# Attention scores gathered ten equally spaced query rows at a time, nine of them used, in blocks of 18 rows

## The chip, the cores and the metric

The kernel runs on one core of a Trainium2 chip. The core has five engines that run side by side and wait for each other by semaphores: TensorE (PE; its weight loads are listed apart as PEld), VectorE (DVE), ScalarE (ACT), GpSimd (POOL) and SyncE (SP). SP computes nothing here: it issues all the transfers, in order, and sixteen DMA engines carry them out. The metric is the device time of one launch in microseconds, lower is better.

## The reference

There are an attention layer whose heads are mixed before and after the softmax, and two expert layers without routing. All is float32; the weights arrive as float64.

```
# B, H, S, D = 4, 12, 448, 64
scores = q @ k.T / sqrt(D)                          # per batch and head
scores = einsum('bhij,hg->bgij', scores, w_pre)     # premix of the heads
attn = exp(scores - max(scores)); attn /= (sum(attn) + 1e-9)
attn = einsum('bhij,hg->bgij', attn, w_post)        # postmix of the heads
x = (attn @ v), heads side by side                  # 1792 tokens x 768
h = x @ w_in;  x = (h * clip(h + 3, 0, 6) / 6) @ w_out          # 768 -> 2048 -> 768
out = ((x @ w1) * (x @ w2)) @ w3 @ moe2_w_out                    # 768 -> 1024 -> 1024 -> 768
```

## The kernel before

Attention goes batch by batch, and in a batch by four chunks of query rows (`CHUNKS`: 120, 100, 116 and 112 rows). `scores` computes a chunk two heads at a time; the result is copied to the tile `s`, in which a partition is a query row and the free dimension is the head and the key. The premix sums over heads, so the heads must come to lie on partitions. That is what the gather is for: a DMA from SBUF to SBUF that takes some query rows of `s`, each with its 12 heads, and lays every pair of row and head on a partition of its own of the tile `g`. One gather of the kernel before takes five rows (four in the short blocks) at equal distance, which is 60 (48) rows of 448 numbers. Four such gathers make a block of 20 (16) query rows: two halves `a_` on the partitions from 0 and from 64 (`PIECE`), and two sides `y` in the free dimension. There are 23 blocks a batch, 92 in all.

In each block `mix(s)` does this. `premix` multiplies the four pieces with `wih`, which holds w_pre on the diagonal of the five rows (`SET`). `rowmax` on DVE takes the maximum, and two exponentials on ACT (`softexp`) write `e` and the sums `z`. `guard`, `recip` and `weigh` scale the postmix weights by one over the sum. `postmix` applies them, with the keys now on partitions (32 small matmuls), and two copies (`evac`, line 283 on DVE, line 281 on ACT) bring the result to `pt`. After two chunks `values` multiplies `pt` with v and stores x in DRAM. The tiles `g`, `e` and the PSUM tiles each have four buffers.

Every engine's order is made by a planner (class `Plan`) while the program is built: each operation has a priority, a guessed duration and its dependencies, and the planner lets every engine take the most urgent operation that is ready in its own list schedule. The numbers that set these priorities stand in `URGE`: `gather=-66.75`, for example, is how far ahead of the block's nominal time (`s * unit0`) a gather stands, and the `p...` numbers say when a second engine may take work of the first. The plan is fixed after that; on the chip each engine works through its list.

The first expert layer begins as the last batch's attention ends. Its weights are loaded by SP, converted from float64 on ACT and DVE, and split into a high and a low part; three matmuls (`product`) make one of float32 precision. Then come the product of w3 and w4 (tile names `w`, `w34`) and the second expert layer (`up`, `down`). All matmuls are issued from line 211, so rows are told apart by their tiles: `sc` scores, `pre` premix, `post` postmix, `val` values, `up` and `dn` the layers.

Of the kernel before, what the change touches and what calls it, by code (L numbers as in the profile page):

```python
# [26 lines left out]

SET = 5
ROWS = 12 * SET
CHUNKS = [[20] * 6, [20] * 5, [20] * 5 + [16], [20] * 4 + [16] * 2]  # L30
LEN = [sum(c) for c in CHUNKS]
CH0 = [sum(LEN[:c]) for c in range(4)]
WIDE = [20 * len(c) for c in CHUNKS]
# [9 lines left out]

def query_order():

    order = np.full(WD0[4], -1)
    for c, blocks in enumerate(CHUNKS):
        c0 = CH0[c]
        for t, n in enumerate(blocks):
            order[WD0[c] + t + len(blocks) * np.arange(n)] = c0 + np.arange(n)  # L50
            c0 += n
    return order
# [3 lines left out]
URGE = dict(pPool=56.7, pACT=727.19, pDVE=31.92, pOut=15.85, pGuard=161.57, pCopy=49.01, pRest=2.09, pEvac=23.46, load0=8.42, load=-2.09, gather=-66.75, pre=-9.2, max=-4.2, exp=24.45, norm=3.85, post=2.04, evac=32.9, values=15.38, step=14.3, vload=27.62, vload0=-34.83, lead=-26.96, begin=-9.0, consts=-93.5, moe=64.56, rows=1.62, win=-43.78, wout=-28.18, w34=16.61, w2=-8.59, unit0=3.751, unit1=12.228, unit2=10.914, w34us=69.106)  # L56
# [146 lines left out]
def attention_moe(ctx: ExitStack, tc, qd, kd, vd, consts, w_in, w_out, w1, w2, w3t, w4, out):  # L203
# [20 lines left out]
    def pool(name, side=left, **kw):  # L224
# [18 lines left out]
        "consts": (cp, [128, 2 * H + SET], F32, 1),  # L243
# [26 lines left out]
    for b in range(B):  # L270
        for c in range(4):
            cstart.append(len(slots))
            for t in range(len(CHUNKS[c])):
                unit_of.append(2 * b + c // 2)
                slots.append((b, c, t))
# [20 lines left out]
    def constants():  # L296
        raw = Buf("consts")
        dma_in(URGE["consts"], consts, raw, ns=300)

        def emit():  # L300
            x = raw.t
            own = x[:, 2 * H:]
# [4 lines left out]
            nc.vector.tensor_tensor(  # L307
                out=wip, in0=x[:, H:2 * H].unsqueeze(2).to_broadcast([128, H, SET]),
                in1=own.unsqueeze(1).to_broadcast([128, H, SET]), op=ALU.mult)
        plan.add("DVE", 700, -6, emit, use=(raw,))  # L310
# [44 lines left out]
    def mix(s):  # L355

        at = s * U0
        b, c, t = slots[s]
        ng, n = len(CHUNKS[c]), CHUNKS[c][t] // 4
        K = 12 * n  # L360
        st = stile[4 * b + c]
        g, pre, m, e, z, r, w, post = (Buf(x) for x in ("g", "pre", "m", "e", "z", "r", "wt", "post"))
        new = [g]
        for a_ in range(2):
            def gather(a_=a_):
                if a_ == 0:
                    take(g)
                for y in range(2):
                    p0 = t + ng * n * (2 * y + a_)
                    nc.sync.dma_start(out=g.t[PIECE * a_:PIECE * a_ + K, y], in_=st.t[p0:p0 + ng * (n - 1) + 1:ng])  # L370
            op = plan.add("SP", 1400, at + URGE["gather"], gather, read=(st,), new=new, after=g.writers[:1], hold=(g,))
            if a_:
                g.writers.append(op)
            new = []
# [7 lines left out]
        plan.add("PE", 950, at + URGE["pre"], premix, use=(g,), new=(pre, e))  # L382
# [37 lines left out]
        def postmix():  # L420
            take(post, *dest)
            for a_ in range(2):
                for k, k0 in enumerate(KEY0):
                    for y in range(2):
                        i, o = slice(PIECE * y, PIECE * y + K), slice(k % 2 * PIECE, (k % 2 + 1) * PIECE)
                        c0 = 256 * a_ + k // 2 * ROWS
                        mm(post.t[o, y, c0:c0 + ROWS], e.t[i, a_, k0:k0 + PIECE], w.t[i, a_], True, True)
        op = plan.add("PE", 1000, at + URGE["post"], postmix, use=(e, w), new=(post, *dest), hold=(pt,), after=() if first else (pt.first,))
        if first:
            pt.first, pt.writers = op, []  # L430

        c0 = CH0[c] - CH0[c // 2 * 2] + sum(CHUNKS[c][:t])
# [5 lines left out]
        for y in range(2):  # L438
            op = plan.add({"ACT": 575, "DVE": 645}, 0, at + URGE["evac"], lambda eng, y=y: evac(eng, y), read=(post,), hold=(pt,), wait="Evac")
# [429 lines left out]
```

## Time and profile before

| what | value |
|---|---|
| time, median of 3 runs | 1405.83 us (1399.33 to 1406.45) |
| the profiled execution | 1406.89 us |
| its span, first to last instruction | 1405.1 us |
| mean granted TensorE clock | 0.967 of full speed |
| PE busy | 1299.0 us, 92% of the span |
| DVE, ACT, POOL busy | 66%, 33%, 26% |
| DMA: moved, share of the 16 engines on the one hardware queue | 155.38 MB, 34.9% |

The shares are averages over unlike stages: attention up to some 430 us, the first expert layer to some 980, then the product of w3 and w4, and the second expert layer. A busy share of PE counts a matmul as long as its record lasts, so it isn't the share of its peak. The DMA share is the mean over sixteen engines: a transfer that sits on a few of them can hold those fully busy and still show as a small share.

### The profile page before, as it was taken

What the parts mean: (1) busy time and instruction counts of PE and PEld (TensorE: products, weight loads), DVE (VectorE), ACT (ScalarE), POOL (GpSimd) and SP (SyncE); (2) the same over time, 40 slices, a digit from 0 to 9 for tenths busy, and PEclk for the clock granted to TensorE, in tenths of its full rate; (3) what the DMA queues carried; (4) which work ended last, traced back from release to release, by engine and by line L of the source; (5) the groups of instructions that cost most, each with busy time, mean ns of one, the idle gap of its engine ahead of it and who ended that gap; (6) DMA issues with size and microseconds to landing.
All of it is one profiled execution on the core that took longest, in us unless ns stands there. A gap on an engine that the chain in (4) does not pass through costs nothing.

```text
span 1405.1 us, 29332 instructions
## 1 busy us (share of the span) xinstructions
PE 1299.0 (92%) x12192; PEld 1040.2 (74%) x12192; DVE 931.4 (66%) x1550; ACT 469.8 (33%) x905; POOL 362.2 (26%) x313
## 2 busy tenths in 40 slices
PE   5898988999889698999999998999998999999998
PEld 2444554555456597888988887998887899999997
DVE  1655656556667698898898989556725665656433
ACT  4544445445445443223222222223314211111110
POOL 0000000000023644343443433323433222222210
PEclk8999999999999799999999999999999999999999
DMA  5354554444455543333233423111623121111004
GB/s 211 134 160 152 157 167 156 153 156 152 155 179 171 186 146 97 107 91 126 91 97 95 123 91 98 53 38 57 192 97 135 46 57 46 45 35 45 23 5 153
DMA packets 75413, 157.26 MB, mean 112 GB/s; under 512 B 7184, under 2 KB 40976, under 8 KB 75280
## 3 DMA queue, kind: packets, MB, share of 16 engines
q1 hardware_dynamic: 75280, 155.38, 34.9%
q8 instruction: 96, 1.57, 0.5%
q14 instruction: 37, 0.30, 0.1%
HBM read 95.32 MB, written 21.50 MB: 83 GB/s over the span
## 4 chain that ended last, share of the span: by engine, by line
PE 43%; DMA 24%; DVE 17%; issue 9%; POOL 4%; SPq 2%; ACT 2%; POOLq 0%; ACTq 0%; DVEq 0%
PE up L211 18%; DMA g<-s 15%; PE dn L211 12%; PE w L211 3%; DVE raw L563 3%; PE pre L211 3%; PE val L211 3%; DVE raw L567 3%; DMA raw<-w 3%; DMA raw<-w_in 2%; PE sc L211 2%; DVE raw L559 2%; DVE raw L565 2%; SPq L370 2%; PE post L211 2%
## 5 line engine op out<-in xcount | busy, mean ns | idle before, releaser
L211 PE MATMUL up<-act,w 128*128 128x448 f32 x2304 | 491.3, 367 | 11.2 <-ACT act L281 3.6
L211 PEld LDWEIGHTS up<-act,w 128*128 128x128 f32 x2304 | 432.7, 189 | 51.5 <-ACT act L281 4.0
L211 PE MATMUL dn<-gs,w 128*128 128x448 f32 x1728 | 384.3, 374 | 31.3 <-POOL gs L214 10.5
L211 PEld LDWEIGHTS dn<-gs,w 128*128 128x128 f32 x1728 | 330.5, 192 | 68.1 <-POOL gs L214 13.9
L652 DVE TENSOR_TENSOR acc<-acc,dn 128x896 f32<-128x896 f32 x168 | 181.4, 1083 | 86.3 <-PE dn L211 83.1
L214 POOL TENSOR_TENSOR gs<-t,gs 128x448 fp32r<-128x448 f32 (+1 forms) x60 | 103.1, 1719 | 316.8 <-ACT gs L281 300.5
L211 PE MATMUL pre<-g,wih 60*64 60x448 f32 (+1 forms) x736 | 138.7, 574 | 36.7 <-DMA g<-s 36.4
L214 POOL TENSOR_TENSOR w<-raw,w 128x768 fp32r<-128x768 f32 (+1 forms) x63 | 125.6, 1995 | 169.7 <-ACT w L281 74.0
L386 DVE TENSOR_REDUCE m<-pre 128x2 f32<-128x896 f32 x92 | 99.7, 1085 | 85.9 <-PE pre L211 85.9
L553 ACT ACTIVATE raw<-raw 128x384 f32<-128x384 f32 (+1 forms) x144 | 75.3, 528 | 241.2 <-DMA raw<-w 102.2
L392 ACT ACTIVATE e<-pre,m 128x448 f32<-128x448 f32 x184 | 115.6, 634 | 83.6 <-DVE m L386 66.0
L211 PEld LDWEIGHTS post<-wt,e 60*64 60x64 f32 (+1 forms) x5888 | 103.2, 136 | 50.8 <-issue 29.3
L211 PE MATMUL post<-wt,e 60*64 60x60 f32 (+1 forms) x5888 | 111.4, 222 | 10.0 <-issue 4.1
L559 DVE TENSOR_SCALAR raw<-raw 128x384 f32<-128x384 f32 (+1 forms) x144 | 78.6, 550 | 63.2 <-ACT raw L553 61.9
L397 POOL TENSOR_SCALAR z<-z 128x2 f32<-128x2 f32 x91 | 19.6, 215 | 391.1 <-ACT e L392 385.7
L283 DVE COPY pt<-post 128x480 f32<-128x480 f32 (+1 forms) x112 | 69.7, 640 | 47.1 <-ACT pt L281 34.7
L281 ACT CAST gs<-t 128x448 fp32r<-128x448 f32 (+1 forms) x59 | 43.6, 739 | 168.3 <-DVE t L809 124.8
L567 DVE SCALAR_TENSOR_TENSOR raw<-raw 128x384 f32<-128x384 uint32 (+1 forms) x144 | 95.4, 666 | 1.2
L211 PEld LDWEIGHTS pre<-g,wih 60*64 60x64 f32 (+1 forms) x736 | 32.3, 137 | 82.7 <-DMA g<-s 73.7
L211 PE MATMUL val<-pt,v 128*64 128x220 f32 (+1 forms) x768 | 88.0, 387 | 4.3 <-ACT e L392 3.3
L563 DVE SCALAR_TENSOR_TENSOR raw<-raw 128x384 int32<-128x384 int32 (+1 forms) x144 | 90.8, 632 | 1.5
L211 PE MATMUL sc<-k,q 64*120 64x448 f32 (+1 forms) x384 | 85.1, 574 | 6.8 <-DMA k<-kd 5.1
(47 smaller groups left out, 1004.1 us busy)
## 6 DMA issues: line engine op xcount, KB each, us to landing
g<-s SPq DMA_DIRECT2D x320, 105.0 KB
raw<-w SPq DMA_DIRECT2D x48, 384.0 KB
v<-vd SPq DMA_DIRECT2D x24, 512.0 KB
raw<-w_in SPq DMA_DIRECT2D x32, 384.0 KB
raw<-w_out SPq DMA_DIRECT2D x32, 384.0 KB
raw<-w3t SPq DMA_DIRECT2D x32, 256.0 KB
raw<-w4dram SPq DMA_DIRECT2D x16, 384.0 KB
k<-kd SPq DMA_DIRECT2D x12, 448.0 KB
```

The source lines that it names most:

```text
L211: nc.tensor.matmul(o, lhsT=lt, rhs=rh, start=start, stop=stop)
L214: eng.tensor_tensor(out=o, in0=a, in1=b, op=ALU.subtract)
L281: nc.scalar.copy(o, i)
L283: nc.vector.tensor_copy(o, i)
L370: nc.sync.dma_start(out=g.t[PIECE * a_:PIECE * a_ + K, y], in_=st.t[p0:p0 + ng * (n - 1) + 1:ng])
L386: nc.vector.tensor_reduce(out=m.t, in_=pre.t[:, :, :S], axis=AX.X, op=ALU.max, negate=True)
L392: nc.scalar.activation(out=e.t[:, a_], in_=pre.t[:, a_, :S], func=ACTF.Exp, bias=m.t[:, a_:a_ + 1], accum_out=z.t[:, a_:a_ + 1])
L553: nc.scalar.mul(value()[:, halves[i]], f(bits(i))[:, :, 1], 2.0 ** -112)
L559: one(out=f(y), in0=f(y), scalar1=F64_TOP, scalar2=-F64_TOP, op0=ALU.min, op1=ALU.max)
L563: two(out=y, in0=hi, scalar=-0x80000000, in1=y, op0=ALU.bitwise_and, op1=ALU.bitwise_or)
L567: two(out=f(hi), in0=lo, scalar=2.0 ** -52, in1=f(hi), op0=ALU.mult, op1=ALU.mult)
L652: nc.vector.tensor_tensor(out=o(), in0=o(), in1=p.t[:, :, :S], op=ALU.add)
```

## The change

A gather now takes ten equally spaced query rows, 120 rows of `g` in one transfer, and the block has two gathers, one for each side `y`. The first five rows lie on partitions 0 to 59. The sixth row (partitions 60 to 71) lies across the border at partition 64 and isn't used by this group; the last four lie on partitions 72 to 119. `wih` gets weights of zero for the sixth row, and the second half of a premix takes partitions 64 to 119. So one group (`GROUP`) is nine query rows, and a block 18. There are 50 groups a batch (the last two have eight rows each), 25 blocks a batch and 100 in all. The distance of the ten rows is the number of groups in the chunk less one (`APART`); by this the sixth row of one group belongs to another: the last group of a chunk, which lies at distance one, is made of the sixth rows (`group_rows`, `query_order`). The chunks have 12, 12, 13 and 13 groups, with 110, 110, 120 and 120 partitions of `s`, and since 37 isn't even, one block a batch takes its two sides from different chunks. The evacuation is cut by half `a_` (five rows of both sides, then four) instead of by side, and its second copy depends on its first in the plan. All numbers of `URGE` have been fitted anew, so the order of every engine changes.

```diff
-CHUNKS = [[20] * 6, [20] * 5, [20] * 5 + [16], [20] * 4 + [16] * 2]
...
+GROUP = 9
+GROUPS = [12, 12, 13, 13]
+APART = [g - 1 for g in GROUPS]
+G0 = [sum(GROUPS[:c]) for c in range(5)]
+BLOCKS = G0[4] // 2
+LEN = [GROUP * g for g in GROUPS[:3]]
+LEN.append(S - sum(LEN))
+WIDE = [10 * d for d in APART]
...
+def group_rows(c, t):
+
+    d = APART[c]
+    return (t, d) if t < d else (5 * d, 1)
...
-URGE = dict(pPool=56.7, pACT=727.19, pDVE=31.92, pOut=15.85, pGuard=161.57, pCopy=49.01, pRest=2.09, pEvac=23.46, load0=8.42, load=-2.09, gather=-66.75, pre=-9.2, max=-4.2, exp=24.45, norm=3.85, post=2.04, evac=32.9, values=15.38, step=14.3, vload=27.62, vload0=-34.83, lead=-26.96, begin=-9.0, consts=-93.5, moe=64.56, rows=1.62, win=-43.78, wout=-28.18, w34=16.61, w2=-8.59, unit0=3.751, unit1=12.228, unit2=10.914, w34us=69.106)
+URGE = dict(pPool=7.45, pACT=670.88, pDVE=510.18, pOut=3.51, pGuard=166.84, pCopy=16.72, pRest=14.77, pEvac=68.05, load0=23.0, load=2.97, gather=-94.67, pre=-13.63, max=-7.21, exp=31.46, norm=6.61, post=2.04, evac=23.77, values=15.1, step=14.3, vload=26.5, vload0=-31.32, lead=-23.93, begin=-9.6, consts=-84.7, moe=45.4, rows=18.18, win=-57.59, wout=-32.41, w34=9.23, w2=4.11, unit0=3.845, unit1=9.887, unit2=10.428, w34us=65.661)
...
-        for a_ in range(2):
-            def gather(a_=a_):
-                if a_ == 0:
+        for y in range(2):
+            G = 2 * t + y
+            c = next(c for c in range(4) if G < G0[c + 1])
+            p0, d = group_rows(c, G - G0[c])
+            st = stile[4 * b + c]
+
+            def gather(y=y, st=st, p0=p0, d=d):
+                if y == 0:
                     take(g)
-                for y in range(2):
-                    p0 = t + ng * n * (2 * y + a_)
-                    nc.sync.dma_start(out=g.t[PIECE * a_:PIECE * a_ + K, y], in_=st.t[p0:p0 + ng * (n - 1) + 1:ng])
-            op = plan.add("SP", 1400, at + URGE["gather"], gather, read=(st,), new=new, after=g.writers[:1], hold=(g,))
-            if a_:
+                nc.sync.dma_start(out=g.t[:120, y], in_=st.t[p0:p0 + 9 * d + 1:d])
+            op = plan.add("SP", 1250, at + URGE["gather"], gather, read=(st,), new=() if y else (g,), after=g.writers[:1], hold=(g,))
+            if y:
                 g.writers.append(op)
...
                 for a_ in range(2):
-                    i, o = slice(PIECE * a_, PIECE * a_ + K), slice(PIECE * y, PIECE * (y + 1))
+                    i, o = slice(PIECE * a_, 120 if a_ else ROWS), slice(PIECE * y, PIECE * (y + 1))
                     mm(pre.t[o, a_, :S], wih[i], g.t[i, y], True, True)
...
-        def evac(eng, y):
-            o = pt.t[:, :, c0 + 2 * n * y:c0 + 2 * n * (y + 1)].rearrange("p c (a i) -> p a c i", a=2)
-            i = post.t[:, y].rearrange("p (a x) -> p a x", a=2)[:, :, :JC * ROWS].rearrange("p a (c i) -> p a c i", i=SET)
-            copy(eng, o, i[:, :, :, :n])
+        def evac(eng, a_):
+            size = GROUP - (t == BLOCKS - 1)
+            n = size - SET if a_ else SET
+            o = pt.t[:, :, c0:c0 + 2 * size].rearrange("p c (y i) -> p y c i", y=2)[:, :, :, SET * a_:SET * a_ + n]
+            i = post.t[:, :, 256 * a_:256 * a_ + JC * ROWS].rearrange("p y (c i) -> p y c i", i=SET)[:, :, :, :n]
+            copy(eng, o, i)
...
+    p = np.arange(128)
+    own = np.where(p < ROWS, p // H, np.where((p < 72) | (p >= 120), -1, (p - 72) // H))
+    own2 = np.where(p % PIECE < ROWS, p % PIECE // H, -1)
```

On SP, in the middle of the first batch, the queue before reads as follows; `g<-s 60x1x448` is a gather of five rows, `x6` six transfers one after the other, and `q`, `k`, `v` are loads from DRAM.

```order
L293 DMA q<-qd 128x600
L370 DMA g<-s 60x1x448 x12
L293 DMA k<-kd 128x896
L370 DMA g<-s 60x1x448 x6
L293 DMA k<-kd 128x896
L370 DMA g<-s 48x1x448 x2
L293 DMA q<-qd 128x720
L370 DMA g<-s 60x1x448 x2
```

At the same place the changed kernel has:

```order
L305 DMA q<-qd 128x660
L381 DMA g<-s 120x1x448 x7
L305 DMA k<-kd 128x896
L381 DMA g<-s 120x1x448 x4
L305 DMA k<-kd 128x896
L381 DMA g<-s 120x1x448 x2
L305 DMA q<-qd 128x720
L305 DMA k<-kd 128x896
```

Of 22 gathers 13 are left in this piece; the loads stand in the same order among them, and the third k load now comes directly behind the q load.

On PE, where attention ends and the first up-projections (`up`) begin, the queue before is this, `pre` and `post` being the mixes of the last blocks and `val` the values:

```order
L211 MATMUL val<-pt,v 64x220 x8
L211 MATMUL up<-act_5607,w 128x448 x6
L211 MATMUL post<-wt,e 64x60 x32
L211 MATMUL up<-act_5607,w 128x448 x6
L211 MATMUL pre<-g,wih 64x448 x4
L211 MATMUL up<-act_5607,w 128x448 x3
```

In the changed kernel it is this:

```order
L224 MATMUL val<-pt,v 64x216 x8
L224 MATMUL pre<-g,wih 64x448 x4
L224 MATMUL post<-wt,e 64x60 x32
L224 MATMUL up<-act_5765,w 128x448 x3
L224 MATMUL pre<-g,wih 64x448 x4
L224 MATMUL up<-act_5765,w 128x448 x6
L224 MATMUL post<-wt,e 64x60 x32
L224 MATMUL up<-act_5765,w 128x448 x3
```

A block's matmuls are the same ones in both (four premixes, 32 postmixes); the up-projections still fill the gaps between the last blocks, now in smaller pieces.

## Rows read from the trace of the kernel before

**Rows 1.** The page: span, and the DMA share in 40 equal slices (tenths).

```profile
span 1405.1 us, 29332 instructions
DMA  5354554444455543333233423111623121111004
```

**Rows 2.** Windows: busy us (instructions) of each engine, granted clock, DMA share, GB/s.

```profile
13.00:427.00 414.00, 364.70 (x7392) 201.09 (x7392) 244.06 (x446) 208.58 (x493) 25.69 (x94) 0.93 0.49 158
50.00:400.00 350.00, 315.97 (x6508) 174.13 (x6508) 210.66 (x383) 176.45 (x415) 16.39 (x77) 0.95 0.49 156
250.00:275.00 25.00, 23.76 (x574) 14.82 (x570) 15.82 (x32) 13.85 (x31) 1.06 (x5) 0.97 0.48 155
300.00:325.00 25.00, 25.00 (x515) 14.87 (x514) 15.27 (x29) 12.83 (x29) 1.06 (x5) 0.88 0.44 142
500.00:880.00 380.00, 358.49 (x1708) 324.03 (x1707) 344.95 (x612) 109.61 (x169) 148.44 (x99) 0.98 0.34 104
```

**Rows 3.** The chain that ended last, by line, as shares of the span.

```profile
PE up L211 18%; DMA g<-s 15%; PE dn L211 12%; PE w L211 3%; DVE raw L563 3%; PE pre L211 3%; PE val L211 3%; DVE raw L567 3%; DMA raw<-w 3%; DMA raw<-w_in 2%; PE sc L211 2%; DVE raw L559 2%; DVE raw L565 2%; SPq L370 2%; PE post L211 2%
```

**Rows 4.** The chain from 200 to 300 us: shares, and one piece (start, us).

```profile
by line: DMA g<-s 47.1%; PE pre L211 12.9%; PE sc L211 10.6%; SPq L370 10.0%; PE val L211 9.4%; PE post L211 8.5%; issue 1.9%; SPq L293 0.5%
...
237.51 8.62 DMA g<-s
```

**Rows 5.** Premix weight loads: the group, and waits from 10 to 60 us.

```profile
L211 PEld LDWEIGHTS pre<-g,wih 60*64 60x64 f32 (+1 forms) x736 | 32.3, 137 | 82.7 <-DMA g<-s 73.7 <-issue 3.1 <-DVE wt L408 2.0
...
PEld pre L211 <- DMA g<-s: 16.3, 12, 8.0
```

**Rows 6.** Windows of the opening loads and of the first gathers.

```profile
0.00:13.00 13.00, 7.86 (x32) 4.03 (x34) 0.42 (x3) 6.38 (x8) 0.19 (x4) 1.00 0.86 306
26.00:32.00 6.00, 6.00 (x29) 1.74 (x26) 3.18 (x4) 2.06 (x6) 0.21 (x1) 0.69 0.33 121
```

**Rows 7.** Timeline of premix weight loads: start, us, what, idle before and releaser.

```profile
26.36 0.29 PEld L211 LDWEIGHTS pre<-g,wih 60*64 60x64 f32 x4 [0.61 <-DMA g<-s]
27.24 0.29 PEld L211 LDWEIGHTS pre<-g,wih 60*64 60x64 f32 x4 [0.59 <-DMA g<-s]
```

**Rows 8.** Gathers: SP's issues (ns min/median/max), then transfers by size.

```profile
L370 SPq DMA_DIRECT2D g<-s x368: 633/742/1071, 13.1 to 427.3; - x184
...
g<-s SPq DMA_DIRECT2D x320, 105.0 KB
...
g<-s SPq DMA_DIRECT2D x48, 84.0 KB
```

**Rows 9.** The chain: two loads from DRAM, one among gathers, one after them.

```profile
315.70 7.53 DMA q<-qd
...
450.96 3.98 DMA v<-vd
```

**Rows 10.** SP's issues in the chain: a gather of 48 rows, a q load.

```profile
210.42 0.63 SPq L370
...
211.84 0.42 SPq L293
```

**Rows 11.** SP's own waits from 50 to 400 us: total us, times, longest.

```profile
SPq L370 <- DMA g<-s: 28.6, 71, 1.1
```

**Rows 12.** The chain: one block's postmix and one premix on PE.

```profile
271.07 1.09 PE post L211 x64
272.16 0.88 PE pre L211 x8
```

**Rows 13.** Evacuations on DVE by form: busy us, mean ns, idle before.

```profile
L283 DVE COPY pt<-post 128x480 f32<-128x480 f32 x95 | 60.7, 655 | 37.5 <-ACT pt L281 27.6 <-PE post L211 9.6
...
L283 DVE COPY pt<-post 128x384 f32<-128x384 f32 x17 | 9.0, 554 | 9.6 <-ACT pt L281 7.1 <-PE post L211 2.5
```

More of the change, by code (lines that the diff above doesn't have):

```diff
@@ L41 @@
 F64_TOP = float(np.array(0x0FEFFFF0, np.uint32).view(np.float32))
+def group_rows(c, t):
+    d = APART[c]
+    return (t, d) if t < d else (5 * d, 1)
 def query_order():
     order = np.full(WD0[4], -1)
[L47 to L51, printed above, removed]
+    for c in range(4):
+        for t in range(GROUPS[c]):
+            first, d = group_rows(c, t)
+            G = G0[c] + t
+            for i, r in enumerate((0, 1, 2, 3, 4, 6, 7, 8, 9)[:GROUP - (G >= G0[4] - 2)]):
+                order[WD0[c] + first + d * r] = GROUP * G - (G == G0[4] - 1) + i
     return order
-URGE = dict(pPool=56.7, pACT=727.19, pDVE=31.92, pOut=15.85, pGuard=161.57, pCopy=49.01, pRest=2.09, pEvac=23.46, load0=8.42, load=-2.09, gather=-66.75, pre=-9.2, max=-4.2, exp=24.45, norm=3.85, post=2.04, evac=32.9, values=15.38, step=14.3, vload=27.62, vload0=-34.83, lead=-26.96, begin=-9.0, consts=-93.5, moe=64.56, rows=1.62, win=-43.78, wout=-28.18, w34=16.61, w2=-8.59, unit0=3.751, unit1=12.228, unit2=10.914, w34us=69.106)
+URGE = dict(pPool=7.45, pACT=670.88, pDVE=510.18, pOut=3.51, pGuard=166.84, pCopy=16.72, pRest=14.77, pEvac=68.05, load0=23.0, load=2.97, gather=-94.67, pre=-13.63, max=-7.21, exp=31.46, norm=6.61, post=2.04, evac=23.77, values=15.1, step=14.3, vload=26.5, vload0=-31.32, lead=-23.93, begin=-9.6, consts=-84.7, moe=45.4, rows=18.18, win=-57.59, wout=-32.41, w34=9.23, w2=4.11, unit0=3.845, unit1=9.887, unit2=10.428, w34us=65.661)
 SHARED = dict(
@@ L270, in attention_moe @@
     for b in range(B):
[L271 to L275, printed above, removed]
+        cstart += [b * BLOCKS + g // 2 for g in G0[:4]]
+        for t in range(BLOCKS):
+            unit_of.append(2 * b + (2 * t >= G0[2]))
+            slots.append((b, t))
     U0 = URGE["unit0"]
@@ L301, in emit @@
             x = raw.t
-            own = x[:, 2 * H:]
+            own, own2 = x[:, 2 * H:2 * H + SET], x[:, 2 * H + SET:]
             nc.vector.memset(wih[:, ROWS:], 0.0)
@@ L308, in emit @@
                 out=wip, in0=x[:, H:2 * H].unsqueeze(2).to_broadcast([128, H, SET]),
-                in1=own.unsqueeze(1).to_broadcast([128, H, SET]), op=ALU.mult)
+                in1=own2.unsqueeze(1).to_broadcast([128, H, SET]), op=ALU.mult)
         plan.add("DVE", 700, -6, emit, use=(raw,))
@@ L379, in premix @@
                 for a_ in range(2):
-                    i, o = slice(PIECE * a_, PIECE * a_ + K), slice(PIECE * y, PIECE * (y + 1))
+                    i, o = slice(PIECE * a_, 120 if a_ else ROWS), slice(PIECE * y, PIECE * (y + 1))
                     mm(pre.t[o, a_, :S], wih[i], g.t[i, y], True, True)
-        plan.add("PE", 950, at + URGE["pre"], premix, use=(g,), new=(pre, e))
+        plan.add("PE", 900, at + URGE["pre"], premix, use=(g,), new=(pre, e))
         def rowmax():
@@ L424, in postmix @@
                     for y in range(2):
-                        i, o = slice(PIECE * y, PIECE * y + K), slice(k % 2 * PIECE, (k % 2 + 1) * PIECE)
+                        i, o = slice(PIECE * y, PIECE * y + ROWS - 12 * a_), slice(k % 2 * PIECE, (k % 2 + 1) * PIECE)
                         c0 = 256 * a_ + k // 2 * ROWS
                         mm(post.t[o, y, c0:c0 + ROWS], e.t[i, a_, k0:k0 + PIECE], w.t[i, a_], True, True)
-        op = plan.add("PE", 1000, at + URGE["post"], postmix, use=(e, w), new=(post, *dest), hold=(pt,), after=() if first else (pt.first,))
+        op = plan.add("PE", 1020, at + URGE["post"], postmix, use=(e, w), new=(post, *dest), hold=(pt,), after=() if first else (pt.first,))
         if first:
             pt.first, pt.writers = op, []
-        c0 = CH0[c] - CH0[c // 2 * 2] + sum(CHUNKS[c][:t])
-        def evac(eng, y):
-            o = pt.t[:, :, c0 + 2 * n * y:c0 + 2 * n * (y + 1)].rearrange("p c (a i) -> p a c i", a=2)
-            i = post.t[:, y].rearrange("p (a x) -> p a x", a=2)[:, :, :JC * ROWS].rearrange("p a (c i) -> p a c i", i=SET)
-            copy(eng, o, i[:, :, :, :n])
-        for y in range(2):
-            op = plan.add({"ACT": 575, "DVE": 645}, 0, at + URGE["evac"], lambda eng, y=y: evac(eng, y), read=(post,), hold=(pt,), wait="Evac")
+        c0 = 2 * GROUP * t - (0 if 2 * t < G0[2] else GROUP * G0[2])
+        def evac(eng, a_):
[4 more added lines that the diff above has]
+            copy(eng, o, i)
+        for a_ in range(2):
+            op = plan.add({"ACT": 575, "DVE": 645}, 0, at + URGE["evac"], lambda eng, a_=a_: evac(eng, a_), read=(post,), after=pt.writers[-1:] if a_ else (), hold=(pt,), wait="Evac")
             pt.writers.append(op)
@@ L839 @@
         vp[:, :, c // 2, c % 2 * PIECE + j0 - k0:c % 2 * PIECE + j1 - k0] = v[:, :, j0:j1]
+    p = np.arange(128)
+    own = np.where(p < ROWS, p // H, np.where((p < 72) | (p >= 120), -1, (p - 72) // H))
+    own2 = np.where(p % PIECE < ROWS, p % PIECE // H, -1)
+    consts = np.concatenate([
+        w_pre[p % H], w_post[p % PIECE % H],
+        *((x[:, None] == np.arange(SET)[None]).astype(np.float32) for x in (own, own2)),
+    ], axis=1)
     def up(w):
```

18 lines of the change are left out of this document (3 added, 15 removed).

## The prediction

> **What bounds the kernel now.** I read the windows by stage first, then the chain of waits, then who waits for the gathered tile, then the DMA rows. The stretch from 13 to 427 us is attention alone: PE is busy for 364.70 of 414 us at a mean granted clock of 0.93, between full speed (2.4 GHz) and half, and the sixteen DMA engines are on average half busy [rows 1, 2]. Behind it come the two expert layers, where PE is already busy for 358.49 of 380 us [rows 2]. The chain that ended last is mostly PE work, but its second line is the gather, 15% of the span, about 216 us [rows 3]. Between 200 and 300 us it is 47.1% of the chain, in pieces of seven to nine microseconds each for a transfer of about 105 KB [rows 4]. PE's weight loads for the premix stood idle 73.7 us for gathers; 16.3 us of that lies in the fill between 10 and 60 us, so 57.4 us come later [rows 5]. That is what the change can reach.
>
> Why does 105 KB take so long while the engines are half idle? The cleanest stretch is 26 to 32 us, with almost nothing but gathers in flight: the DMA share is 0.33, which is 5.3 of 16 engines, and they move 121 GB/s. The opening loads reach 0.86, or 13.8 engines, and 306 GB/s [rows 6]. Per busy engine both give 22 to 23 GB/s. In the same stretch PE's premixes start 0.88 us apart, each of these steps waiting for one more gather [rows 7]: 107.5 KB (105.0 in units of 1024) in 0.88 us is 122 GB/s, the same rate. So the gathers run on about five engines at those engines' full speed, and five is the number of query rows that one gather names in its source. Loads queue behind them: a q load takes 7.53 us at 315 us, while a larger v load takes 3.98 us once gathers have ended [rows 9].
>
> The whole stage agrees. The gathers move 320 times 105.0 KB and 48 times 84.0 KB [rows 8], 38.5 MB. The stage moves 158 GB/s for 414 us, 65.4 MB [rows 2], so 26.9 MB are other traffic. On five engines gathers put 7.7 MB on each; the rest, over sixteen, adds 1.7. That is 9.4 MB at 23 GB/s, 409 us of the 414. DMA and PE bound the stage together, DMA a little more.
>
> **The change part by part.** *Gathers.* 368 transfers become 200 of 120 rows, 215 KB each: 43.0 MB, 4.5 MB more, because one of ten rows is not used. A gather now names ten source rows. If the split follows that number, each of ten engines carries 4.3 + 1.7 = 6.0 MB, 261 us at 23 GB/s: well under PE, so the wait goes. If it stays at five, 8.6 + 1.7 = 10.3 MB, 448 us, which is 39 us more than before. The trace before has only four and five source rows, so it can't show ten; I take ten, because 5.3 busy engines lie close to the number of rows named. The wider split stops binding at six engines: 43.0/n + 1.7 = 9.0 MB (390 us) gives n = 5.9.
>
> The Trainium skill's page "DMA: Bandwidth & Descriptors", section "Why a DMA increments its semaphore by 16 and not by 1", says that a transfer is split over the largest number up to 16 that divides the slowest dimension of both access patterns. By that rule the count is 5 before (5 and 60) and 10 after (10 and 120); the trace agrees with the 5, and no run here shows the 10. The same page's "Rules for kernel authors" says that two transfers to disjoint partition halves use the same 16 engines, and that one whole transfer should take their place. Taken alone, it would make the DMA time of this change only the 11.7% of extra bytes. The share of 0.33 speaks against all 16 being in use.
>
> *SP's queue.* Issuing a gather holds SP 0.742 us at the median [rows 8]; one of 48 rows takes 0.63 [rows 10], and about 0.04 us lies between issues. That is 0.009 us a row; extended to 120 rows it is 1.28 us. With no growth it is 0.74, at double 1.48. So 200 gathers cost SP 156 to 304 us, by my value 264, against 320 × 0.78 + 48 × 0.67 = 282 now. Some 90 other transfers at 0.42 + 0.04 [rows 10] add 41 us. SP would be at 305 of some 380 us: no bound, but close enough to give waits of its own. SP's present waits for earlier gathers, 28.6 us between 50 and 400 [rows 11], go too.
>
> *The fill.* The first block's second half is SP's fifth gather instead of its ninth: 5 × 1.32 = 6.6 us instead of 9 × 0.78 = 7.0. The next three blocks follow at one gather of 1.32 us each instead of two at 0.88. That is 2 us gained; the rest of the 16.3 us stands.
>
> *Eight more blocks.* 100 blocks replace 92, each with the same premix and postmix: 0.88 us and 1.09 us on PE [rows 12], 1.97 us; eight are 15.8 us on the path. Scores and values keep their counts; their widths move by ten query rows of 120 in two of four chunks and by four columns in 228, and the 448 columns that a scores matmul streams stay.
>
> *Evacuation.* A block's two copies are now 480 and 384 elements a partition in place of 480 and 480: 0.655 and 0.554 us on DVE [rows 13], 0.1 us saved where the second is the last thing before values, else hidden behind the next premix on PE. Already now the copies follow one another (the DVE one waits for ACT's [rows 13]), so the planner's new dependency adds no wait. The setup's slightly wider constants are a single load hidden behind the q and k loads. A block that straddles two chunks needs the next chunk's scores one block earlier; these are issued well ahead, and all scores on the chain are 2% of the span [rows 3], 28 us over 16 chunks, so without that cover it costs under 2 us a batch.
>
> *The refitted planner.* In the expert layers PE's order keeps its pattern. PE has only 380 − 358.49 = 21.5 us idle from 500 to 880 [rows 2], which caps the gain there; I take 0 and allow 8 either way. Where attention ends, first up-projections still interleave with the last postmixes.
>
> **The sum.** Two readings of how much wait goes. By waits: 57.4 and 2 us gone, 15.8 added, −43.6. By busy share: the stretches 250 to 275 and 300 to 325 us, when gathers had run ahead, have PE busy 23.76 and 25.00 of 25, 97.5%; (364.70 + 15.8)/0.975 = 390 in place of 414, −24. Between them I take −34: once the gathers are early, PE meets the softmax chain and SP instead, but a higher clock should give some back. The profiled execution took 1406.9 us (span 1405.1 [rows 1] and 1.8 around it), so 1373; it stands 1.1 above the median of 1405.8, so **1372 us**.
>
> The Trainium skill's page "Perfetto Trace Analysis", section "Identifying the Most-Contended Engine", says that matmul busy time hides headroom and that the busy share of weight loads is the better measure. Here they are busy 201.09 of 414 us [rows 2], 49%; by that PE has slack, and the reading by waits, 1363, would be the better one.
>
> **The rivals.** *The split stays at five engines* (chance 0.07). For it: the trace never shows more for a gather. Against it: 0.33 of the DMA share with five rows named. The added 39 us of engine time show as even longer gathers in the chain: 1445. It decides below six engines.
>
> *The wait moves* (0.14). The gather comes early, and PE waits instead for rowmax, exponentials or free PSUM. For it: DVE is busy 210.66 and ACT 176.45 of 350 us [rows 2], 60% and 50%, and 8.7% more blocks in less time makes that some 70% and 60% in a chain of dependent steps; SP is near 80%. Against it: at 97.5% PE those same engines kept up. If only about 16 of the 57.4 us come back, the change is even: 1405, from 1396 up.
>
> *The new order costs the expert layers* (0.05): a weight converted late behind the shorter attention stage leaves PE idle where DVE is busy 344.95 of 380 us [rows 2]. DVE's work there doesn't shrink with attention. If the 34 us of earlier start are given back, plus 8: 1414.
>
> **How the numbers follow.** My forecast has 0.74, with 1346 to 1395 as its own range: 1363 less the clock's share (0.93 to 0.97 over 414 us is 17 us) and 1383 plus 12 for SP and the order. About 0.5% (7 us) is what a measurement of this kernel can tell from no change. Faster takes the 0.74 and 0.06 of the second rival; same takes 0.08 of that and 0.02 of the third; slower keeps the split at five and the rest. The range, 1346 to 1403, leaves out the first and the third rival and the upper end of the second.
>
> **What would show it.** Right: the premix's idle for gathers falls from 73.7 to below 30 us, gather pieces in the chain shorten to three or four microseconds, in the fill the DMA share rises above 0.45 with gathers alone, attention ends near 395 us instead of 427, the stretch behind it keeps its length. Wrong: a DMA share of a third in the fill again; SP issues of over 1.5 us; or PE as idle as before, released by DVE or ACT.

## The result and the profile after

The changed kernel takes 1363.12 us (median of 4 runs, 1356.27 to 1368.38) against 1403.68 for the kernel before (4 runs, the three above and one more): a ratio of 0.971, 95% interval 0.966 to 0.977. The forecast was 1372 within 1346 to 1403. The profiled execution took 1356.27 us, the fastest of the four and 7 us below the median, so its stages are together some 7 us short.

The page, span, DMA share and granted clock in 40 slices:

```profile
span 1354.5 us, 30391 instructions
DMA  7566766666755233333333331303624112110003
PEclk8999999999996989899999999999999999999999
```

Windows of the stages (busy us and instructions of PE, PEld, DVE, ACT, POOL, then clock, DMA share, GB/s), answering to [rows 2]; the gathers now end at 372 us instead of 427:

```profile
13.00:372.00 359.00, 338.70 (x7886) 199.33 (x7882) 257.65 (x464) 219.53 (x542) 29.20 (x102) 0.97 0.66 195
50.00:350.00 300.00, 293.42 (x6964) 173.25 (x6958) 221.35 (x395) 184.56 (x459) 17.70 (x83) 0.99 0.66 195
450.00:820.00 370.00, 344.58 (x1626) 311.38 (x1625) 324.44 (x582) 108.88 (x166) 149.14 (x94) 0.97 0.33 103
```

PE is busy for 97.8% of the stage's steady part, the DMA share has gone from 0.49 to 0.66, and the mean clock from 0.93 to 0.97. The chain from 200 to 300 us, by line and in a few of its pieces (start, us), holds no gather any more; before, gathers were 47.1% of it [rows 4]:

```profile
by line: PE post L224 29.0%; PE sc L224 27.5%; PE pre L224 23.2%; PE val L224 19.2%; issue 1.5%
...
207.34 1.69 PE sc L224 x8
209.03 2.02 PE post L224 x128
211.06 1.51 PE pre L224 x16
212.56 0.67 PE post L224 x43
```

The premix's weight loads between 10 and 60 us, and all issues of gathers on SP (ns min/median/max, first and last start), against [rows 5, 8]:

```profile
PEld pre L224 <- DMA g<-s: 8.1, 4, 6.4
...
L381 SPq DMA_DIRECT2D g<-s x200: 768/799/2837, 13.5 to 372.6; - x100
```

The 8.1 us, all in the fill, are now the whole wait of these loads for gathers; it was 73.7. The matmuls of the premix waited for gathers too, in part at the same time: 36.4 us before, 6.4 now. And a gather of 120 rows holds SP hardly longer, by the median, than one of 60 did (0.799 against 0.742 us).

Where the time went, by the first and last starts of matmuls in the two profiled executions:

| | before | after | difference |
|---|---|---|---|
| last premix | 437.7 us | 379.8 us | −57.9 |
| first down-projection (`dn`) | 473.3 | 416.3 | −57.0 |
| last down-projection | 1400.1 | 1349.5 | −50.6 |

So attention gave 58 us, and the expert layers took 6 to 7 back. This is one execution of each kernel: between these two lie 50.6 us, between the medians 40.6.

### The profile page after: what moved, and what is told of

Its sections match the earlier page's. It is cut to its first block, busy times and chain, and to the rows that moved or that the text cites. A ratio compares the mean times of both kernels' runs of the same rounds, so it can differ in the third digit from the quotient of the medians.

```text
span 1354.5 us, 30391 instructions
## 1 busy us (share of the span) xinstructions
PE 1279.9 (94%) x12768; PEld 1042.9 (77%) x12768; DVE 951.9 (70%) x1574; ACT 481.9 (36%) x955; POOL 366.5 (27%) x319
## 4 chain that ended last, share of the span: by engine, by line
PE 58%; DVE 17%; issue 9%; DMA 8%; POOL 4%; ACT 2%; SPq 1%; POOLq 0%; ACTq 0%; DVEq 0%
PE up L224 19%; PE dn L224 11%; PE post L224 7%; PE pre L224 6%; PE sc L224 6%; PE val L224 6%; PE w L224 3%; DVE raw L579 3%; DVE raw L575 3%; DVE raw L571 2%; DMA raw<-w 2%; DMA raw<-w_out 2%; DVE raw L577 2%; DVE acc L664 2%; DMA raw<-w_in 1%
## 5 line engine op out<-in xcount | busy, mean ns | idle before, releaser
L227 POOL TENSOR_TENSOR gs<-t,gs 128x896 fp32r<-128x896 f32 (+1 forms) x64 | 111.0, 1734 | 353.4 <-ACT gs L293 352.3
L402 ACT ACTIVATE e<-pre,m 128x448 f32<-128x448 f32 x200 | 125.7, 637 | 35.2 <-DVE m L396 27.4
L396 DVE TENSOR_REDUCE m<-pre 128x2 f32<-128x896 f32 x100 | 107.0, 1086 | 36.1 <-PE pre L224 35.4
L224 PE MATMUL post<-wt,e 60*64 60x60 f32 (+1 forms) x6400 | 113.8, 221 | 10.3 <-issue 7.5
L293 ACT CAST gs<-t 128x896 fp32r<-128x896 f32 (+1 forms) x64 | 48.3, 755 | 184.7 <-DVE t L821 124.0
L224 PE MATMUL pre<-g,wih 60*64 60x448 f32 (+1 forms) x800 | 99.9, 577 | 10.0 <-DMA g<-s 6.4
L579 DVE SCALAR_TENSOR_TENSOR raw<-raw 128x384 f32<-128x384 uint32 (+1 forms) x144 | 102.7, 718 | 1.1
L224 PE MATMUL sc<-k,q 64*120 64x448 f32 (+1 forms) x384 | 93.5, 586 | 5.2 <-DMA k<-kd 5.2
L293 ACT CAST w<-raw 128x768 fp32r<-128x768 f32 (+1 forms) x54 | 42.2, 781 | 116.7 <-DVE raw L575 42.1
L293 ACT COPY pt<-post 128x384 f32<-128x384 f32 (+2 forms) x107 | 59.1, 566 | 65.3 <-PE post L224 40.4
L224 PE MATMUL val<-pt,v 128*64 128x216 f32 (+1 forms) x768 | 81.0, 363 | 0.1
```

The lines of the kernel that those rows point to most:

```text
L224: nc.tensor.matmul(o, lhsT=lt, rhs=rh, start=start, stop=stop)
L227: eng.tensor_tensor(out=o, in0=a, in1=b, op=ALU.subtract)
L293: nc.scalar.copy(o, i)
L396: nc.vector.tensor_reduce(out=m.t, in_=pre.t[:, :, :S], axis=AX.X, op=ALU.max, negate=True)
L402: nc.scalar.activation(out=e.t[:, a_], in_=pre.t[:, a_, :S], func=ACTF.Exp, bias=m.t[:, a_:a_ + 1], accum_out=z.t[:, a_:a_ + 1])
L579: two(out=f(hi), in0=lo, scalar=2.0 ** -52, in1=f(hi), op0=ALU.mult, op1=ALU.mult)
```

## The experiments

Each timed kernel was measured beside the kernel before, whose median was 1405.1, 1405.8 or 1405.6 us there, and the ratios are to that. The theory: a gather sits on as many DMA engines as it names source rows, these engines bound the attention stage before, and after the change PE does. The rivals: the count of transfers and SP's time to issue them; the planner's new numbers.

### Gathers alone

The kernel does nothing but gathers of one shape after the other from a tile of zeros, for example:

```
phase("five", lambda g: nc.sync.dma_start(out=g[:], in_=s[0:4 * 11 + 1:11]), 60)
phase("ten", lambda g: nc.sync.dma_start(out=g[:], in_=s[0:9 * 11 + 1:11]), 120)
phase("sixteen", lambda g: nc.sync.dma_start(out=g[:], in_=s[0:15 * 7 + 1:7, :7]), 112)
```

> Nothing of the reference is computed here (the output is zeros): 32 gathers of each shape alone, eight in flight, to measure the disputed cost by itself. Theory (a gather runs on as many engines as it names source rows, each at 22 to 24 GB/s): four rows 95 GB/s, five rows 120 GB/s, eight rows 190 GB/s, ten rows 230 GB/s, so that a gather of 215 KB lands every 0.9 to 1.0 us; DMA share 0.25, 0.31, 0.50, 0.62. Rival (SP's issue grows with the rows, 1.28 us for 120 of them): ten rows no more than 165 GB/s, SP never waiting. Rival (all gathers use the same engines): 120 GB/s for every shape. In the fill of the changed kernel SP took 0.80 us a gather, so the first rival already looks weak; the sixteen-row shape tells whether more engines still help, or SP is then the limit at about 250 GB/s.

Windows with five, ten, four, eight rows, ten rows of half the keys, ten neighbouring and sixteen rows (the last three columns are clock, DMA share, GB/s):

```profile
15.00:55.00 40.00, 0.00 (x0) 0.00 (x0) 1.00 0.22 64
65.00:105.00 40.00, 0.00 (x0) 0.00 (x0) 1.00 0.47 129
120.00:160.00 40.00, 0.00 (x0) 0.00 (x0) 1.00 0.19 51
175.00:215.00 40.00, 0.00 (x0) 0.00 (x0) 1.00 0.37 103
222.00:245.00 23.00, 0.00 (x0) 0.00 (x0) 1.00 0.47 129
260.00:345.00 85.00, 0.00 (x0) 0.00 (x0) 1.00 0.52 62
362.00:386.00 24.00, 0.00 (x0) 0.00 (x0) 1.00 0.68 221
```

The rate is proportional to the rows named, 12.8 to 13 GB/s for each of four, five, eight and ten and 13.8 for sixteen, so the rival that has all shapes on the same engines falls. SP's shortest issue of ten rows was 0.77 us in the third kernel below, so the rival of an issue that grows to 1.28 us falls too. A rate in proportion to the rows is also a fixed time for each gather, some 1.63 us here for four to ten rows; that reading falls in the third kernel, where a gather of five rows takes 0.81 us and one of ten 1.13 or 1.36. But the rate is little more than half of what the fill of the kernel before showed, so the size was open. Two more such kernels tried it. In the second, successive gathers read different rows.

```
phase(f"turn{n}", lambda g, t, n=n: nc.sync.dma_start(out=g[:], in_=s[t:t + (n - 1) * 11 + 1:11]), 12 * n)
```

> Nothing of the reference is computed (the output is zeros): 44 gathers of each shape alone, sixteen in flight, and now successive gathers read different rows of the source, as in the attention stage. The run with the same rows each time gave 13 GB/s for each row named (51, 64, 103, 129 GB/s for 4, 5, 8, 10 rows), where the fill of the kernel before has 23 to 24. If that was one partition being read again and again: 22 to 24 GB/s for each row here, 118 for five, 190 for eight, and for ten 215 to 235 or SP's issue, 265; same5 stays at 64. If the fill's rate had another reason: 13 GB/s for each row again. Ten neighbouring rows (near10) stay at 62 GB/s by either. The first sixteen issues of each shape wait for nothing and give SP's time: 0.63 us for four rows, 0.74 for five, 0.77 for ten were seen so far; if that is set by the count of rows, two rows lie below 0.55 and eight between 0.74 and 0.77.

Windows with four, five, eight and ten rows:

```profile
70.00:110.00 40.00, 0.00 (x0) 0.00 (x0) 1.00 0.20 57
135.00:170.00 35.00, 0.00 (x0) 0.00 (x0) 1.00 0.28 73
180.00:220.00 40.00, 0.00 (x0) 0.00 (x0) 1.00 0.42 116
245.00:300.00 55.00, 0.00 (x0) 0.00 (x0) 1.00 0.55 147
```

That is 14.3 to 14.7 GB/s a row: reading the same rows again was not the reason. In this kernel ten neighbouring rows, a different ten each time, gave 113 GB/s instead of the 62 of the first. The third kernel set the distance of the rows to six, as in three of the four chunks before, and to five for ten rows, and let successive gathers read one partition on (beside) or 60 on (apart).

```
phase("beside", lambda g, i: nc.sync.dma_start(out=g[:], in_=s[i % 6:i % 6 + 25:6]), 60)
phase("apart", lambda g, i: nc.sync.dma_start(out=g[:], in_=s[i // 2 % 6 + i % 2 * 60:i // 2 % 6 + i % 2 * 60 + 25:6]), 60)
```

> Nothing of the reference is computed (the output is zeros): gathers alone again, sixteen in flight. With sources in turn, one partition further each time, five rows gave 73 GB/s and ten 143, some 15 GB/s a row. In the kernel before two successive gathers read rows 60 partitions apart. If that is why its fill reached 121 GB/s: apart gives 110 to 125 GB/s and beside 70 to 80, for ten rows (tenapart) 200 or more against 140 (tenbeside). If not, apart and beside are alike, and the difference to the kernel has another reason.

Windows: five rows beside and apart, ten beside and apart, two rows, sixteen rows:

```profile
10.00:40.00 30.00, 0.00 (x0) 0.00 (x0) 1.00 0.33 124
45.00:75.00 30.00, 0.00 (x0) 0.00 (x0) 1.00 0.33 126
85.00:135.00 50.00, 0.00 (x0) 0.00 (x0) 1.00 0.57 159
142.00:185.00 43.00, 0.00 (x0) 0.00 (x0) 1.00 0.58 192
192.00:222.00 30.00, 0.00 (x0) 0.00 (x0) 1.00 0.13 50
228.00:255.00 27.00, 0.00 (x0) 0.00 (x0) 1.00 0.94 273
```

Two things follow. The first is the number of engines. In this third kernel the DMA share is 2.1 engines for two rows, 5.3 for five, 9.2 for ten and 15.0 for sixteen: the number of engines is the number of source rows, as the rule in the Trainium skill's page "DMA: Bandwidth & Descriptors" (section "Why a DMA increments its semaphore by 16 and not by 1") gives it for these shapes, and now for ten as well.

The share is a mean of busy time and can come out lower (3.5 engines for five rows and 7.5 for ten in the first kernel), so a second reading helps: the trace has the start and the duration of every packet. Packets of 1792 bytes under way at once are two for 90% of the time with two rows and five for 77% with five; with ten rows ten is the most frequent count (33 and 36%). In the kernel before, from 26 to 32 us, they are five for 79%.

The second is that the rate of a row depends on where the rows lie: five rows six partitions apart reach 124 GB/s with or without the jump of 60 (SP starts one every 0.81 us, which allows little more, 132), eleven apart 73. My guess, the jump, was wrong for five rows; for ten it gives a fifth more. Why the distance counts is not settled. For the change it means that a gather on ten engines, at the distance of 11 that two of its four chunks have, carries 147 GB/s alone, not the 230 of my sum; the distance of 12 in the other two wasn't measured alone.

### The same bytes on five engines again

```diff
-                nc.sync.dma_start(out=g.t[:120, y], in_=st.t[p0:p0 + 9 * d + 1:d])
+                for r in range(0, 10, 5):
+                    nc.sync.dma_start(out=g.t[12 * r:12 * r + 60, y], in_=st.t[p0 + r * d:p0 + (r + 4) * d + 1:d])
```

> The changed kernel with each gather of ten rows cut into two of five rows; nothing else differs, and it issues 400 gathers. Theory (engines): five engines carry 43.0/5 + 1.7 = 10.3 MB each, 448 us at 23 GB/s, so the last premix comes near 455 us instead of 380 and the time is 1415 to 1445 us; the premix's idle for gathers is above 60 us again. Rival (the new order of the planner made the gain): within 15 us of 1363. Rival (fewer transfers, each with a fixed cost): slower, but by as much as the next run, which issues as many.

1485.25 us, a ratio of 1.054 (1.049 to 1.059) to the kernel before. The order is that of the changed kernel, so the refit alone can't have made the gain. The premix's weight loads wait 100.1 us for gathers. The five engines carry 10.3 MB each in the 490 us from first to last gather, 21.0 GB/s. Do two such gathers run on different engines? No: from 100 to 450 us more than seven packets of 1792 bytes are under way for less than 0.1% of the time, and five is the most frequent count (47%), where the uncut kernel has ten. The time is more than I expected. The five rows lie 11 or 12 partitions apart here, not six as in the kernel before, and alone such gathers reached 73 GB/s instead of 124; the stage's clock fell to 0.88 as well. How much each adds isn't separated. Its window:

```profile
14.00:504.00 490.00, 430.99 (x7940) 229.66 (x7940) 260.33 (x467) 221.28 (x545) 29.18 (x103) 0.88 0.46 143
```

### As many transfers, on ten engines

```diff
-                nc.sync.dma_start(out=g.t[:120, y], in_=st.t[p0:p0 + 9 * d + 1:d])
+                for k in range(0, S, S // 2):
+                    nc.sync.dma_start(out=g.t[:120, y, k:k + S // 2], in_=st.t[p0:p0 + 9 * d + 1:d, :, k:k + S // 2])
```

> The changed kernel with each gather cut into two of ten rows and half the keys: 400 gathers, as in the run before, but ten source rows in each. Theory (engines): the same bytes on ten engines, so PE stays the bound; SP issues 400 x 0.80 + 41 = 361 us in some 370, which may cost a little: 1360 to 1385 us. Rival (number of transfers): as slow as the cut by rows, 1415 or more.

1410.46 us, ratio 1.002 (1.000 to 1.005). Both expectations missed. With as many transfers it is 75 us faster than the cut by rows, which is what the ten engines are worth there. It is 47 slower than the uncut kernel, so the count of transfers matters too: with 400 of them, ten engines gain nothing on the kernel before. Its stage:

```profile
14.00:426.00 412.00, 369.00 (x7953) 215.28 (x7952) 260.26 (x467) 221.56 (x545) 29.05 (x102) 0.95 0.60 169
```

SP is issuing for 400 of the 412 us between the first and the last gather: 329 for the 400 gathers, some of them held longer than the median of 0.769, 47 for 70 other transfers, the rest gaps. In the kernel with half the bytes below, SP is issuing for nearly the same share, 319 of 332 us, without harm. Half gathers alone reached 129 GB/s in the first kernel of this study, 333 us for 43.0 MB, with the loads still to come. Whether SP or the transfers held it at 412 isn't separated.

### Eight rows and two

```diff
-                nc.sync.dma_start(out=g.t[:120, y], in_=st.t[p0:p0 + 9 * d + 1:d])
+                for r, n in ((0, 8), (8, 2)):
+                    nc.sync.dma_start(out=g.t[12 * r:12 * (r + n), y], in_=st.t[p0 + r * d:p0 + (r + n - 1) * d + 1:d])
```

> The changed kernel with each gather cut into one of eight rows and one of two. Theory (a gather of n rows sits on the first n engines): the first two engines get 24 rows of 1792 bytes from each pair, as many as each of the first five gets from two gathers of five, so the time is that of the cut five and five within 15 us, although eight engines share the work. Rival (it is the number of engines, or the mean load, that counts): nearer to the uncut kernel, 1365 to 1390 us.

1444.61 us, ratio 1.027 (1.024 to 1.030): 41 us faster than five and five, not within 15, and 81 slower than uncut. If the first two engines take a row of both parts, they carry 8.6 + 1.7 = 10.3 MB in 446 us, 23.1 GB/s. Put beside the kernel before (9.4 MB in 414 us, 22.7) and five and five (21.0), the busiest engine runs at 21 to 23 GB/s in all three, although the DMA share is 0.46 to 0.51:

```profile
14.00:460.00 446.00, 404.35 (x7935) 221.43 (x7935) 260.36 (x467) 221.10 (x544) 29.40 (x103) 0.92 0.51 156
```

The packets bear out that the two parts share engines: from 100 to 450 us eight are under way at once for 17% of the time, ten or more for 2%, so the gather of two rows has no engines of its own beside the eight. Which engines these are the trace doesn't say, and the 9% between the two cuts are not explained.

### Half the bytes, before and after

```diff
-                    nc.sync.dma_start(out=g.t[PIECE * a_:PIECE * a_ + K, y], in_=st.t[p0:p0 + ng * (n - 1) + 1:ng])
+                    nc.sync.dma_start(out=g.t[PIECE * a_:PIECE * a_ + K, y, :S // 2], in_=st.t[p0:p0 + ng * (n - 1) + 1:ng, :, :S // 2])
...
-                    mm(pre.t[o, a_, :S], wih[i], g.t[i, y], True, True)
+                    mm(pre.t[o, a_, :S], wih[i], g.t[i, y, :S // 2].unsqueeze(1).to_broadcast([K, 2, S // 2]), True, True)
```

> The kernel before with gathers that carry only the first half of the keys (224 of 448); each premix matmul reads that half twice, so PE has the same columns and the scores of the second half are replaced by the first. The issues stay 368, five engines, half the bytes. If the bytes on five engines bound the attention stage: (7.7/2 + 1.7) MB at 23 GB/s are 241 us, so SP's 323 us and PE take over, the last premix comes 30 to 45 us earlier than 437 and the time is 1358 to 1375 us. If SP's issues bound it: no gain, 1395 or more. If both, as the cut by keys of the changed kernel suggests: about half of that, 1378 to 1392.

1323.81 us, ratio 0.939 (0.936 to 0.942): 82 us less, more than any of the three. The bytes on the five engines were the bound, with the same 368 issues and the old order. Its stage:

```profile
13.00:344.00 331.00, 311.48 (x7358) 184.87 (x7358) 241.94 (x445) 207.95 (x491) 25.46 (x93) 0.99 0.44 138
```

The waits of the premix's loads for gathers fell from 73.7 to 14.2 us. The clock is 0.99 where it was 0.93. Before, it was at half speed for 54.6 us of the stage, and PE was busy in 44.3 of these, which costs at most 22 us; here that is under 2. So some 60 us of waits and 20 of clock make up about the 82. This is an estimate, since a part of both may be the same time.

The same cut in the changed kernel is the control.

> The changed kernel with gathers of the first half of the keys, which each premix matmul reads twice (the scores of the second half are replaced by the first): the control to the same cut in the kernel before, which gave 82 us. If DMA no longer bounds attention: within 8 us of 1363. If the gathers still bound it in part: 1345 or less.

1348.66 us, ratio 0.958 (0.954 to 0.962), some 14 us less than the changed kernel; neither of the two expectations. The gain lies in the fill. Windows of this kernel:

```profile
13.00:46.00 33.00, 25.88 (x486) 12.78 (x485) 17.98 (x33) 21.37 (x49) 1.70 (x8) 0.95 0.43 114
50.00:350.00 300.00, 292.94 (x6988) 172.99 (x6990) 227.01 (x407) 189.64 (x472) 24.40 (x88) 1.00 0.50 142
```

In the changed kernel PE had issued 346 matmuls from 13 to 46 us, at a clock of 0.79:

```profile
13.00:46.00 33.00, 21.99 (x346) 10.81 (x346) 12.40 (x22) 16.48 (x37) 1.21 (x5) 0.79 0.56 159
```

From 50 to 350 us both do the same work (6988 and 6964 matmuls, PE busy 293 of 300). So in the steady part the gathers bound nothing any more. The last premix comes at 368.1 us, 12 earlier, and the 140 matmuls that it is ahead at 46 us, two blocks, are most of that.

### The planner's numbers

The changed kernel with all numbers of before, then the kernel before with all the new ones. The edit is the two lines of `URGE` in the change's diff, exchanged.

> The changed kernel with the numbers of the planner of before. Theory (the shape of the gathers makes the gain): 1355 to 1385 us, attention ends within 15 us of where the changed kernel's does. Rival (the refit makes it): 1395 us or more.

1378.96 us, ratio 0.979 (0.973 to 0.984). The last premix comes at 403.2 us, 23 later than with the new numbers, more than the 15 I had allowed.

> The kernel before with the refitted numbers and nothing else. Theory: no gain, 1395 to 1425 us. Rival (the refit makes the gain): 1385 us or less.

1413.37 us, ratio 1.005 (1.003 to 1.007). The new numbers alone cost half a percent; with the new gathers they are worth 16 us by the medians, though the two intervals (0.979 and 0.971) still touch. They seem to fit the new shape rather than the kernel as such.

The changed kernel with the old numbers for the expert layers alone, twelve entries of `URGE`:

```diff
-pPool=7.45, pCopy=16.72, pRest=14.77, moe=45.4, rows=18.18, win=-57.59, wout=-32.41, w34=9.23, w2=4.11, unit1=9.887, unit2=10.428, w34us=65.661
+pPool=56.7, pCopy=49.01, pRest=2.09, moe=64.56, rows=1.62, win=-43.78, wout=-28.18, w34=16.61, w2=-8.59, unit1=12.228, unit2=10.914, w34us=69.106
```

> The changed kernel with the planner's numbers of before for the expert layers alone (moe, rows, win, wout, w34, w2, unit1, unit2, w34us, and the thresholds pPool, pCopy, pRest). The change ended attention 58 us earlier and the whole 51 us, so the expert layers gave 7 us back. If that is the new numbers' doing: 1350 to 1358. If the layers follow from when attention ends, whatever the numbers: 1360 to 1372. If the old numbers don't fit the new end of attention: over 1372.

1351.95 us, ratio 0.961 (0.958 to 0.964): faster than both kernels, and the interval lies below the changed kernel's. Attention is unchanged (last premix at 379.5 us). From the first to the last `dn` the layers take 925.2 us, against 933.2 with the new numbers, 926.8 before, and 925.5 in the changed kernel with all numbers old. The matmuls of `dn` (ns min/median/max, first and last start):

```profile
L224 PE MATMUL dn<-gs,w x1728: 358/366/741, 416.2 to 1341.4; 128*128 128x448 f32 x192
```

So the loss behind attention doesn't follow from attention's earlier end: the old numbers undo it. But the new numbers don't cost it everywhere: in the kernel before they take 922.7 us from the first to the last `dn`, the least of all, and in the run with pairs below 925.5. The loss comes from these numbers together with the order in which the changed kernel leaves attention; which of the twelve makes it isn't shown.

### Blocks in pairs

```diff
-        at = s * U0
+        at = s // 2 * 2 * U0
```

> The changed kernel with the priorities of two successive blocks made equal, so that premixes and postmixes come two at a time more often. PE is busy 97.8% of the attention stage now; two premixes in a row take 1.51 us, one alone 0.91, two postmixes 2.02, one alone 1.09. If PE's changes from one kind to another are what is left: up to 0.3 us saved in two blocks' premix and 0.16 in their postmix, for half the blocks more than now some 10 us: 1350 to 1358. If the pairs make PE wait for the softmax chain instead: 1365 to 1390.

1368.20 us, ratio 0.972 (0.968 to 0.976), not told apart from the changed kernel. Attention ends later (last premix at 392.7 us), PE is busy 274.52 instead of 293.42 of the 300 us from 50 on. The time lies where the second expectation had it, but what PE waits for wasn't followed up. Pairs don't help in this form.

## Why the prediction was right, and where its sizes were off

*What bounded the kernel.* Right. The five engines' load explained the stage, and halving the bytes alone gave 82 us with the issues and the order left as they were.

*Ten source rows, ten engines.* Right in kind: the share of 9.2 engines for ten rows shows it, and cutting the rows in two on the same order cost 122 us, of which 75 remain against as many transfers on ten engines. The size was off: I gave each engine 23 GB/s, 261 us for the stage. At the change's spacing ten rows carry 147 GB/s alone, which makes 43.0 MB 293 us. That is an estimate from one distance (in the kernel cut five and five a row got 17.5 GB/s, more than the 14.7 here), but it is still under PE's 339, so the step held. The rule in the section "Rules for kernel authors" of the Trainium skill's page "DMA: Bandwidth & Descriptors", that two transfers to disjoint halves share the same 16 engines, holds here in part: gathers of five rows occupy 5.3 engines, not 16, but two of them do share these, and one transfer in their place paid.

*SP's queue.* The extrapolation by rows was wrong: 0.80 us for 120 rows by the median, not 1.28. The other transfers in the stage are 70, not some 90. So SP needs 200 × 0.84 + 70 × 0.46 = 200 us, not 305; since some issues were held longer (all 200 took 197 us), it was occupied for some 258 of 360. Nothing hung on it here, because SP wasn't the bound. What the sum left out is that the count of transfers could be a bound: 400 on ten engines took back the gain.

*The fill.* 2 us were counted. The last start of the weight loads of the first four blocks' premixes moved from 31.7 to 28.8 us, and the waits for gathers in it from 16.3 to 8.1 us. The fill is where the gathers still cost something, some 12 us.

*Eight more blocks.* 15.8 us were counted; a premix is 0.91 us now and a postmix 1.09, 16.0 for eight.

*The sum.* The range held, and the reading by waits (1363) was the nearer of the two, but that 1372 came within 9 us is in part luck. From the profiled execution of before I took −34. Attention gave 58, the expert layers took 7 back, and the two profiled executions lie 10 us further apart than the medians.

The reading by busy share (−24) was too careful, because it took the 364.70 us for work of PE. The run with half the bytes has the same matmuls and is busy for 311.48 us. The premix alone shows it, in the kernel before and in that run (us of PE busy, matmuls, then clock, DMA share, GB/s):

```profile
13.00:427.00 414.00, 136.78 (x720) 0.93 0.49 158
...
13.00:344.00 331.00, 94.59 (x720) 0.99 0.44 138
```

So some 53 of the 364.70 us were no work at full speed: half the clock and, it seems, matmul records that lasted through waits. The busy share of the weight loads, 49%, had spoken for the reading by waits; it was still only 58% (173.25 of 300) in the steady part after, where PE was the bound all the same, so it doesn't tell where PE's limit lies.

By parts, as an estimate: 57.4 us of gather waits and 3 of the fill gone; of the clock at most 22 us before (44.3 us busy at half speed) and at most 8 after (16.4 us), so 14; 16 added. Together that is −58, against −57.9 measured at the last premix. The parts may overlap, so the agreement doesn't prove each of them. The clock, which I had left to the lower end of the range, was thus the second gain after the waits.

*The refit.* I took 0 with 8 either way for the expert layers. They lost 6 to 8 us, a small part of the third rival, and the old numbers there win them back.

*The rivals.* Five engines would indeed have been slower: 1485 us, 40 more than my price, though that run also issues twice as many transfers. The wait that moves to SP or the softmax chain did not come.

*The signs.* Those for being right came: 8.1 us of waits for gathers (below 30), no gather in the chain from 200 to 300 us, the last gather at 372 us (395 was expected), and a DMA share above 0.45 in the fill:

```profile
26.00:32.00 6.00, 4.53 (x26) 1.33 (x21) 4.71 (x7) 3.91 (x13) 0.51 (x2) 0.63 0.48 125
```

The stretch behind didn't keep its length, by the 7 us above. One sign of being wrong came in part without harm: 21 of the 200 issues took over 1.5 us.

## What to carry to other kernels

When transfers are slow and the DMA share is low, multiply the share by sixteen in a stretch with one kind of transfer: a number near the size of the transfer's outer source dimension tells that its shape, not its bytes, holds it back. The share is a mean, so it can come out below the count; the packets under way at once are the safer reading. A transfer that names more rows may then move more bytes and still win, as long as each engine's share of the bytes takes well less time than the compute behind it, and as long as the number of transfers doesn't grow with it. A gain read from waits should be given the clock's share as well when the waits kept the clock down, and when a planner is fitted anew for one stage, the other stages' numbers deserve a run of their own.

## What the runs showed of the hardware that was not expected

- SP's time to issue a gather hardly follows its rows: 0.62 us for 24 rows of two partitions, 0.63 for 48 of four, 0.74 for 60 of five, 0.77 for 120 of ten and 0.57 for 112 rows of sixteen (the shortest issues). A load of 120 rows from DRAM takes 0.32.
- Two gathers of five source rows, one after the other, run on the same five engines: at most seven packets are under way at once (but for 0.1% of the time), where with gathers of ten rows ten is the most frequent count.
- The distance of the source rows changes the rate: five rows six partitions apart 124 GB/s, eleven apart 73, the same five again and again 64. Ten neighbouring rows, the same each time, 62 GB/s, although the share says 8.3 engines are occupied.
- The granted clock of the attention stage followed the waits: 0.88 with five engines in the new order, 0.93 before, 0.97 after, 0.99 with half the bytes.
